# Sliding-window attention on one core: pairs of scores with banks of their own, maxima in two halves

## The chip, the core and the metric

The kernel runs on one core of a Trainium2 chip, as one launch. Its time is the device time of that core in microseconds. A core has a matmul engine (PE, with its weight loads shown apart as PEld), a vector engine (DVE), an activation engine (ACT), a general one (POOL), and a queue that issues transfers (SP). Matmuls write PSUM, a small memory of eight banks of 512 fp32 columns in 128 partitions; DVE and ACT read it. All other tiles lie in SBUF.

## The reference

`x` has 2048 tokens of 512 features. Its layernorm `xn` goes two ways: through attention with 32 heads of 16 features, in which a token sees itself and the 255 tokens before it, and through a mixer block that gates the result. The attention part, from the reference:

```python
qkv = (x @ wqkv).reshape(B, S, 3, H, Dh)            # B=1, S=2048, H=32, Dh=16; x is layernorm(A_x)
scores = einsum("bhqd,bhkd->bhqk", q, k) * Dh ** -0.5
mask = (i - j >= 0) & (i - j < 256)
p = softmax(where(mask, scores, -1e9))
o = einsum("bhqk,bhkd->bhqd", p, v)
s = o.transpose(0, 2, 1, 3).reshape(B, S, D) @ wo
g = silu(gelu(layernorm(x) @ w1 + b1) @ w2 + b2)
out = A_x + s * g
```

## The kernel before

The program has three stages. The first (to about 67 us) normalises and transposes `x` and projects the first heads. The second is the attention loop. The third, after it, is the mixer's second matmul, the output projection and the gate.

The attention loop works on groups of four heads (8 groups, `n`), in blocks of 128 tokens (16 blocks a group). One step `t` of the loop is one block of one group, so steps 0 to 127. Four heads are two **pairs** `p`; the two heads of a pair, `a` = 0 and 1, lie in two halves of 64 partitions. A step has these parts, in this order on PE:

- `prob_block(..., 1)`: scores of pair 1, keys by queries, two matmuls of up to 384 columns, one a head, into the two banks of the tile `stb`. ACT takes the exponential of both (one instruction on 128x768 elements) into `pt`, and POOL masks its two edges (`affine_select`).
- `max_block`: for the block 12 steps ahead (`LEAD`), scores the other way round, queries by keys, to get each query's maximum: four matmuls of 256 columns into the two banks of `xy` (the nearer keys) and four of 128 into columns 0 to 255 of the two banks of `zo` (the farthest block, which only counts where the nearest is masked). The first two blocks of a group have no farthest block and use a constant. DVE puts the masked elements in place (`copy_predicated`, reading `zo`, writing `xy`) and takes the maximum over `xy` (`tensor_reduce`) into `mt`. Every fourth step `max_rows` sends the maxima through DRAM into the rows of the queries, so that a later step's scores come out with the maximum taken off.
- `fill_in(t, 0)`: the first half of this step's **fill**, matmuls that have nothing to do with the step: projections of later groups, values, hidden units of the mixer. They write the banks `fb`. Most steps have six matmuls of 512 columns (or twelve of 256) here.
- planned pieces of other engines (`plan`): casts, splits, fetches.
- `prob_block(..., 0)`: the same for pair 0, again into `stb`.
- `fill_in(t, 1)`: the second half of the fill, between none and twelve matmuls.
- `pv_step`: for the block before, the values: up to 24 small matmuls into the 128 columns `otb`, which are columns 256 to 383 of the second bank of `zo`. ACT copies them out (`oraw`).

Four things hold the order. Each engine works through its instructions in the order in which the program wrote them. `Ordered` (its call is line 42, which all instructions therefore bear in the profile) keeps it so. Waits are put in by the tile layer, by PSUM bank: two engines are never in the same bank of a tile at once, whichever columns they use. And a tile's instructions wait for each other only through the engines' counters; a counter's value names one instruction of that engine.

In the last 12 steps no maxima are left to take, and pair 1's scores use `xy` instead of `stb`.

Of the kernel before, what the change touches and what calls it, by code (L numbers as in the profile page):

```python
# [23 lines left out]
NQ = H // 4  # L24
EPS = 1e-5
NEG = -3.0e38
LEAD = 12
# [22 lines left out]
def mixer_kernel(ctx, tc, x, wqk, wv, wo, w1, b1, w2, b2, out):  # L50


    nc = SimpleNamespace(**{name: Ordered(tc, name) for name in ("tensor", "vector", "scalar", "gpsimd", "sync")})
# [130 lines left out]

    xy = psum.tile([P, 2, 512], F32, name="xy")
    zo = psum.tile([P, 2, 512], F32, name="zo")
    otb = zo[:, 1, 256:384]
    psf = attn.enter_context(tc.tile_pool(name="psf", bufs=1, space=PSUM))
    fb = [psf.tile([P, 512], F32, name=f"fb{i}") for i in range(2)]
    early = ExitStack()  # L190
# [1 line left out]
    stb = []  # L192
# [7 lines left out]
    vt = vp.tile([P, NKB, 16, DH + 1], F32, name="vt")  # L200
# [16 lines left out]
    upper = const.tile([P, P], F32, name="upper")  # L217
    mhalf = const.tile([P, 4], F32, name="mhalf")
    negc = const.tile([P, 1], F32, name="negc")
    nc.vector.memset(upper, 1.0)  # L220
    nc.vector.memset(otb, 0.0)
    for _ in range(16):
        nc.tensor.matmul(zo[:, 0, 0:P], upper, upper, start=True, stop=True)
    nc.gpsimd.memset(mhalf, -0.5)
# [2 lines left out]
    nc.vector.memset(negc, NEG)  # L227
    mask = upper.bitcast(I32).unsqueeze(1).unsqueeze(1).to_broadcast([P, 2, 2, P])
    neg = negc.unsqueeze(2).unsqueeze(2).to_broadcast([P, 2, 2, P])
    b1s = const.tile([P, NF], F32, name="b1s")  # L230


# [234 lines left out]

    mts = {}

    def max_block(n, qb):  # L470

        slot = slots[n % 2]
        if qb % 4 == 0:
# [4 lines left out]
        def scores(p, a, first):  # L478
            r = slice(64 * a, 64 * a + 64)
            out, keys = ((zo[:, a, P * p: P * (p + 1)], slice(P * (qb - 2), P * (qb - 1))) if first else  # L480
                         (xy[:, a, 256 * p + off: 256 * (p + 1)], slice(P * lo, P * (qb + 1))))
            nc.tensor.matmul(out, slot[r, 0, p, P * qb: P * (qb + 1)], slot[r, 1, p, keys], start=True, stop=True)

        for p, a, first in ((0, 1, False), (0, 0, False), (1, 1, False), (1, 0, False),
                            (0, 1, True), (0, 0, True), (1, 1, True), (1, 0, True)):
            if qb >= 2 or not first:
                scores(p, a, first)
        four = xy.rearrange("q a (p k) -> q a p k", p=2)
        nc.vector.copy_predicated(four[:, :, :, 128:256], mask,
                                  neg if qb < 2 else zo[:, :, 0:256].rearrange("q a (p k) -> q a p k", p=2))  # L490
        nc.vector.tensor_reduce(out=mts[n, qb // 4][:, :, :, qb % 4],
                                in_=four[:, :, :, off:256],
                                axis=AX.X, op=ALU.max, negate=True)

    def max_rows(n, c, t):
# [15 lines left out]
    def prob_block(n, kb, p):  # L511
        slot = slots[n % 2]
        w = min(384, S - P * kb)
        pt = pp.tile([P, 2, 384], F32, tag="pt", name=f"pt_{n}_{kb}_{p}")
        both = xy if p and 16 * n + kb + LEAD >= 16 * NQ else stb[0]
        for a in (1, 0):
            r = slice(64 * a, 64 * a + 64)
            nc.tensor.matmul(both[:, a, 0:w], slot[r, 1, p, P * kb: P * (kb + 1)],
                             slot[r, 0, p, P * kb: P * kb + w], start=True, stop=True)
        nc.scalar.activation(pt[:, :, 0:w], both[:, :, 0:w], AF.Exp, scale=DH ** -0.5)  # L520
        nc.gpsimd.affine_select(out=pt[:, :, 0:P], in_=pt[:, :, 0:P], pattern=[[0, 2], [1, P]],
                                compare_op=ALU.is_ge, fill=0.0, base=0, channel_multiplier=-1)
        if w == 384:
            nc.gpsimd.affine_select(out=pt[:, :, 256:384], in_=pt[:, :, 256:384],
                                    pattern=[[0, 2], [-1, P]], compare_op=ALU.is_gt, fill=0.0,
                                    base=0, channel_multiplier=1)
        pts[(n, kb, p)] = pt


    outs = {}  # L530

    def pv_step(n, qb):

        lo = max(qb - 2, 0)
        for kb in range(lo, qb + 1):
            for j in range(4):
                nc.tensor.matmul(otb[32 * j: 32 * j + DH + 1], vt[:, kb, (4 * n + j) % 16],
                                 pts[n, kb, j // 2][:, j % 2, P * (qb - kb): P * (qb - kb + 1)],
                                 start=(kb == lo), stop=(kb == qb),
                                 skip_group_check=True, tile_position=(0, 32 * j))  # L540
        if qb % 4 == 0:
            outs[0] = sgp.tile([P, 512], F32, tag="or", name=f"oraw_{n}_{qb}", bufs=2)
        nc.scalar.copy(outs[0][:, P * (qb % 4): P * (qb % 4 + 1)], otb)
        if qb % 4 == 3:
            (at if n or qb > 7 else behind)(16 * n + qb + 2, nc.sync.dma_start, oT_d[n // 2, n % 2::2, :, P * (qb - 3): P * (qb + 1)], outs[0])

# [228 lines left out]
    def fill_in(t, half):  # L775
        now[:] = t, half
        run(delayed.pop((t, half), ()))
        for fn, args in fills.get((t, half), ()):
            fn(*args)

    end = 16 * NQ
    for t in range(-16, end + 1):
        m = t + LEAD
        if t == -5:
            open_slot(1)
            for k in range(4):
                at(-4 + k, clear_part, k)
        if 0 <= t < end:
            if t == 0:
                early.close()  # L790
                stb.append(attn.enter_context(tc.tile_pool(name="ps_s2", bufs=1, space=PSUM)).tile(
                    [P, 2, 512], F32, name="stb"))
            prob_block(t // 16, t % 16, 1)
        if t >= 0 and m < end:
            max_block(m // 16, m % 16)
        fill_in(t, 0)
        for fn, args in plan.get(t, []):
            fn(*args)
# [12 lines left out]
        for fn, args in ends.get(t, []):  # L811
            fn(*args)
# [20 lines left out]
    for f in range(6, NF, 2):  # L833
        t = gp.tile([P, 2, 512], F32, tag="ohl", name=f"hr_{f}", bufs=4)
# [185 lines left out]
    for c in range(2):  # L1020
# [23 lines left out]
        for i in range(NF + 1):  # L1044
# [47 lines left out]
            k = i - o_from  # L1092
# [163 lines left out]
```

## Time and profile before

| | |
|---|---|
| time, median of 3 runs | 767.51 us (766.88 to 767.55) |
| time of the profiled execution | 767.48 us |
| span of the profiled execution | 765.8 us |
| PE busy, weight loads busy | 745.3 us, 581.8 us |
| DVE, ACT, POOL busy | 526.4, 437.3, 292.3 us |
| first scores of step 0 | 67.22 us |
| first scores of step 116 | 412.24 us |
| end of the last step | about 439.25 us |
| granted PE clock | 1.00 in all stretches |

Idle time of an engine means little by itself here. What counts is which instruction each engine waits for. The span leaves out what lies before the first and after the last profiled instruction (1.7 us here).

### The profile page before, as it was taken

To read this page: it belongs to the slowest core of one execution; us is meant where nothing else is said; L and a number is where in the kernel's file an instruction comes from. 1 tells how busy PE (TensorE), PEld (TensorE's weight loads), DVE (VectorE), ACT (ScalarE), POOL (GpSimd) and SP (SyncE) were. 2 spreads that over 40 slices of the span, in tenths; PEclk is the share of its full clock that TensorE was granted. 3 is DMA by queue.
4 is the path that set the end of the run, shared out by engine and by line. 5 is a ranking of instruction groups with operands and counts; after the bars stand their busy time and mean duration, and the time that the engine had idled before them with its cause. 6 is when DMAs were issued, how large, how long until landed. Compare 5 with 4: busy or idle time off the path is not lost.

```text
span 765.8 us, 18809 instructions
## 1 busy us (share of the span) xinstructions
PE 745.3 (97%) x7428; PEld 581.8 (76%) x7428; DVE 526.4 (69%) x833; ACT 437.3 (57%) x742; POOL 292.3 (38%) x595
## 2 busy tenths in 40 slices
PE   9899999999999999999999999999999999999997
PEld 8777676766768887676676688888878888888886
DVE  6786776877777778887874447753657665676373
ACT  7736767867666676777877755444644553442001
POOL 7612566666565554766766700030101100001102
PEclk9999999999999999999999999999999999999999
DMA  7723455656447863555735283541202322253531
GB/s 261 208 45 75 94 128 137 155 116 134 98 98 219 248 204 98 117 143 145 197 114 155 59 293 120 178 152 56 69 28 93 100 92 81 77 163 115 177 96 55
DMA packets 56951, 99.40 MB, mean 130 GB/s; under 512 B 11104, under 2 KB 11360, under 8 KB 56864
## 3 DMA queue, kind: packets, MB, share of 16 engines
q1 hardware_dynamic: 56864, 98.21, 45.2%
q8 instruction: 58, 0.95, 0.5%
q14 instruction: 29, 0.24, 0.1%
HBM read 51.39 MB, written 29.62 MB: 106 GB/s over the span
## 4 chain that ended last, share of the span: by engine, by line
PE 87%; ACT 4%; DVE 4%; issue 2%; POOL 2%; DMA 1%; SPq 0%; DVEq 0%; ACTq 0%; POOLq 0%
PE acc L42 19%; PE fb L42 18%; PE zo L42 13%; PE p L42 9%; PE stb L42 8%; PE h L42 6%; PE s L42 6%; PE xy L42 5%; ACT pt L42 3%; PE pv L42 2%; DMA x<-in_x_dram 1%; DVE xy L42 1%; DVE mt L42 1%; POOL pt L42 1%; PE yt L42 1%
## 5 line engine op out<-in xcount | busy, mean ns | idle before, releaser
L42 POOL TENSOR_SCALAR_AFFINE_SELECT pt<-pt 128x256 f32<-128x256 f32 x480 | 192.8, 426 | 161.5 <-ACT pt L42 160.4
L42 ACT ACTIVATE pt<-stb 128x768 f32<-128x768 f32 (+1 forms) x244 | 188.6, 773 | 55.5 <-PE stb L42 46.1
L42 DVE TENSOR_REDUCE mt<-xy 128x4 f32<-128x1024 f32 (+1 forms) x128 | 152.6, 1192 | 4.4
L42 PE MATMUL acc<-w,gh 128*128 128x512 f32 x432 | 134.6, 393 | 0.0
L42 DVE COPY_PREDICATED xy<-upper,zo 128x512 f32<-128x512 int32 x112 | 77.5, 692 | 69.1 <-PE zo L42 68.4
L42 PE MATMUL fb<-xnT,wqb 64*128 64x512 f32 (+1 forms) x684 | 115.2, 404 | 0.8 <-DVE xnT L42 0.8
L42 PE MATMUL zo<-pt,vt 128*17 128x128 f32 x2880 | 103.9, 275 | 1.8 <-DVE xy L42 1.3
L42 PE MATMUL stb<-qk 64*128 64x384 f32 (+1 forms) x488 | 96.7, 392 | 7.4 <-ACT pt L42 5.9
L42 POOL TENSOR_TENSOR xo<-xo,gated 128x512 f32<-128x512 f32 x15 | 20.2, 1347 | 219.0 <-DVE gated L42 215.2
L42 PEld LDWEIGHTS zo<-pt,vt 128*17 128x17 f32 x2880 | 67.5, 97 | 39.0 <-issue 17.8
L42 PEld LDWEIGHTS acc<-w,gh 128*128 128x128 f32 x432 | 80.9, 188 | 17.2
L42 PEld LDWEIGHTS stb<-qk 64*128 64x128 f32 x488 | 45.5, 183 | 52.9 <-ACT pt L42 41.6
L42 PE MATMUL acc<-w,gl 128*128 128x512 f32 x216 | 84.4, 391 | 0.0
L42 PEld LDWEIGHTS fb<-xnT,wqb 64*128 64x128 f32 (+1 forms) x684 | 63.4, 186 | 7.8 <-DVE xnT L42 1.2
L42 PE MATMUL xy<-qk 64*128 64x256 f32 (+2 forms) x536 | 61.5, 303 | 2.2 <-DVE mt L42 2.0
L42 ACT COPY oraw<-zo 128x128 f32<-128x128 f32 x128 | 34.1, 266 | 40.2 <-PE zo L42 35.5
L42 PEld LDWEIGHTS xy<-qk 64*128 64x128 f32 x536 | 43.9, 185 | 13.6 <-DVE mt L42 7.1
L42 PEld LDWEIGHTS acc<-w,gl 128*128 128x128 f32 x216 | 40.5, 188 | 9.3 <-DVE gl L42 0.2
L42 ACT ACTIVATE gated<-acc 128x512 f32<-128x512 f32 x16 | 8.7, 595 | 64.8 <-DVE acc L42 64.8
L42 PE MATMUL s<-wos,ohl 128*128 128x512 f32 (+1 forms) x204 | 44.8, 378 | 0.0
L42 PEld LDWEIGHTS s<-wos,ohl 128*128 128x128 f32 x204 | 36.7, 188 | 7.1
L42 ACT COPY p<-p 128x512 f32<-128x512 f32 x21 | 12.3, 584 | 50.1 <-PE p L42 42.6
(190 smaller groups left out, 1191.2 us busy)
## 6 DMA issues: line engine op xcount, KB each, us to landing
qk<-sh SPq DMA_DIRECT2D x128, 128.0 KB
qk<-pjr SPq DMA_DIRECT2D x64, 128.0 KB
oT_d<-oraw SPq DMA_DIRECT2D x32, 256.0 KB
w_d<-in_w_dram SPq DMA_DIRECT2D x14, 512.0 KB
x<-in_x_dram SPq DMA_DIRECT2D x16, 256.0 KB
or<-oT_d SPq DMA_DIRECT2D x16, 256.0 KB
w<-rden_d SPq DMA_DIRECT2D x16, 256.0 KB
xo<-in_x_dram SPq DMA_DIRECT2D x16, 256.0 KB
```

Of the source, the lines that this page charges most:

```text
L42: r = issue(*args, **kwargs)
```

## The change

Three things change in the loop, in all steps from 0 on.

1. Pair 0's scores go to `zo`, columns 0 to 383 of both banks; pair 1's stay in `stb`, in the last 12 steps too.
2. The values go to columns 384 to 511 of the first bank of `stb`, and ACT copies them from there. The memset that clears these columns once stands at step 0, no more at the start.
3. The maxima of a step are taken in two halves, one for each pair (`max_half`): pair 0's where `max_block` stood, pair 1's behind pair 0's scores. Each half is two matmuls into its half of `xy`, two into columns 384 to 511 of both banks of `zo`, a masked copy of half the size and a reduction of half the size. `max_block` remains for the 12 blocks that are done before step 0, with its columns of `zo` moved to 256 to 511.

```diff
-    otb = zo[:, 1, 256:384]
...
-    nc.vector.memset(otb, 0.0)
...
+    mask1 = upper.bitcast(I32).unsqueeze(1).to_broadcast([P, 2, P])
+    neg1 = negc.unsqueeze(2).to_broadcast([P, 2, P])
...
-    def max_block(n, qb):
+    def max_scores(n, qb, places):
...
+        for first in range(1 + (qb >= 2)):
+            for p, firsts in places:
+                for a in (1, 0):
+                    r = slice(64 * a, 64 * a + 64)
+                    out, keys = ((zo[:, a, firsts: firsts + P], slice(P * (qb - 2), P * (qb - 1))) if first else
+                                 (xy[:, a, 256 * p + off: 256 * (p + 1)], slice(P * lo, P * (qb + 1))))
+                    nc.tensor.matmul(out, slot[r, 0, p, P * qb: P * (qb + 1)], slot[r, 1, p, keys],
+                                     start=True, stop=True)
+        return off
...
+    def max_half(n, qb, p):
+
+        off = max_scores(n, qb, ((p, 384),))
+        two = xy[:, :, 256 * p: 256 * (p + 1)]
+        nc.vector.copy_predicated(two[:, :, 128:256], mask1, neg1 if qb < 2 else zo[:, :, 384:512])
+        nc.vector.tensor_reduce(out=mts[n, qb // 4][:, :, p, qb % 4], in_=two[:, :, off:256],
                                 axis=AX.X, op=ALU.max, negate=True)
...
-        both = xy if p and 16 * n + kb + LEAD >= 16 * NQ else stb[0]
+        both = stb[0] if p else zo
...
-                nc.tensor.matmul(otb[32 * j: 32 * j + DH + 1], vt[:, kb, (4 * n + j) % 16],
+                nc.tensor.matmul(stb[0][32 * j: 32 * j + DH + 1, 0, 384:512], vt[:, kb, (4 * n + j) % 16],
...
-        nc.scalar.copy(outs[0][:, P * (qb % 4): P * (qb % 4 + 1)], otb)
+        nc.scalar.copy(outs[0][:, P * (qb % 4): P * (qb % 4 + 1)], stb[0][:, 0, 384:512])
...
+                nc.vector.memset(stb[0][:, 0, 384:512], 0.0)
             prob_block(t // 16, t % 16, 1)
         if t >= 0 and m < end:
-            max_block(m // 16, m % 16)
+            max_half(m // 16, m % 16, 0)
         fill_in(t, 0)
...
             prob_block(t // 16, t % 16, 0)
+        if t >= 0 and m < end:
+            max_half(m // 16, m % 16, 1)
         fill_in(t, 1)
```

How this stands on the engines is shown at three places of step 10. The first is PE from pair 1's scores (the two `stb<-qk` of 384 columns) on: `xy<-qk` and `zo<-qk` of 128 columns are the maxima's, `zo<-pt` the values. The names in brackets are the engines' counters that a matmul waits for. Before:

```order
L42 MATMUL stb<-qk_91 128x384 [waits Activation_49]
L42 MATMUL stb<-qk_91 128x384
L42 MATMUL xy<-qk_706 128x256 [waits DVE_49]
L42 MATMUL xy<-qk_706 128x256 x3
L42 MATMUL zo<-qk_706 128x128 [waits Activation_49]
L42 MATMUL zo<-qk_706 128x128 x3
L42 MATMUL fb_108<-xnT,wqb_1164 128x512
...
L42 MATMUL stb<-qk_91 128x384 [waits Activation_49]
L42 MATMUL stb<-qk_91 128x384
...
L42 MATMUL zo<-pt_8_0_1269,vt 17x128 [waits DVE_49]
```

And in the changed kernel:

```order
L42 MATMUL stb<-qk_91 128x384 [waits Activation_49]
L42 MATMUL stb<-qk_91 128x384
L42 MATMUL xy<-qk_705 128x256 [waits DVE_49]
L42 MATMUL xy<-qk_705 128x256
L42 MATMUL zo<-qk_705 128x128 x2
L42 MATMUL fb_108<-xnT,wqb_1172 128x512
...
L42 MATMUL zo<-qk_91 128x384 [waits DVE_49]
L42 MATMUL zo<-qk_91 128x384
L42 MATMUL xy<-qk_705 128x256 [waits DVE_49]
L42 MATMUL xy<-qk_705 128x256
L42 MATMUL zo<-qk_705 128x128 [waits Activation_49]
L42 MATMUL zo<-qk_705 128x128
```

Before, pair 0's scores waited for ACT, namely for the exponential of pair 1 of the same step. Now they wait for DVE (the first half's masked copy). Behind them the second half has moved in, and its `zo` matmuls wait for ACT, namely for the exponential that reads pair 0's scores.

The second place is PE at the end of the step, from the last values (`<-pt,vt`) to the next step's first scores. Before:

```order
L42 MATMUL zo<-pt_10_0_1363,vt 17x128 [waits Pool_49]
L42 MATMUL zo<-pt_10_0_1363,vt 17x128
L42 MATMUL zo<-pt_10_1_1341,vt 17x128 x2
L42 MATMUL stb<-qk_91 128x384 [waits Activation_49]
L42 MATMUL stb<-qk_91 128x384
```

In the changed kernel:

```order
L42 MATMUL stb<-pt_10_0_1379,vt 17x128 [waits Pool_49]
L42 MATMUL stb<-pt_10_0_1379,vt 17x128
L42 MATMUL stb<-pt_10_1_1361,vt 17x128 x2
L42 MATMUL stb<-qk_91 128x384 [waits Activation_49]
L42 MATMUL stb<-qk_91 128x384
```

The order is the same, but the two now share a tile: the scores' wait for ACT was for the exponential of pair 0 of the step before, and is now for the copy `oraw` of the values just written.

The third place is ACT in the same step. Before:

```order
L42 COPY oraw_8_1335<-zo 128x128 [waits DMAHW1_49,DVE_49,PE_49]
L42 ACTIVATE pt_10_1_1341<-stb 128x768 [waits PE_49,Pool_49]
L42 ACTIVATE pt_10_0_1363<-stb 128x768 [waits PE_49]
L42 COPY oraw_8_1335<-zo 128x128 [waits DVE_49,PE_49]
L42 ACTIVATE pt_11_1_1384<-stb 128x768 [waits PE_49,Pool_49]
```

In the changed kernel:

```order
L42 COPY oraw_8_1355<-stb 128x128 [waits DMAHW1_49,PE_49]
L42 ACTIVATE pt_10_1_1361<-stb 128x768 [waits PE_49,Pool_49]
L42 ACTIVATE pt_10_0_1379<-zo 128x768 [waits DVE_49,PE_49]
L42 COPY oraw_8_1355<-stb 128x128 [waits PE_49]
L42 ACTIVATE pt_11_1_1406<-stb 128x768 [waits PE_49,Pool_49]
```

ACT's order is unchanged. The copy of the values no longer waits for DVE, and the exponential of pair 0 now does.

More of the change, by code (lines that the diff above doesn't have):

```diff
@@ L468, in mixer_kernel @@
     mts = {}
-    def max_block(n, qb):
+    def max_scores(n, qb, places):
         slot = slots[n % 2]
-        if qb % 4 == 0:
+        if qb % 4 == 0 and places[0][0] == 0:
             mts[n, qb // 4] = small.tile([P, 2, 2, 4], F32, tag="mt", name=f"mt_{n}_{qb}")
@@ L476, in max_block @@
         off = 128 * (lo + 1 - qb)
[L478 to L487, printed above, removed]
+        for first in range(1 + (qb >= 2)):
[7 more added lines that the diff above has]
+        return off
+    def max_block(n, qb):
+        off = max_scores(n, qb, ((0, 256), (1, 384)))
         four = xy.rearrange("q a (p k) -> q a p k", p=2)
         nc.vector.copy_predicated(four[:, :, :, 128:256], mask,
-                                  neg if qb < 2 else zo[:, :, 0:256].rearrange("q a (p k) -> q a p k", p=2))
+                                  neg if qb < 2 else zo[:, :, 256:512].rearrange("q a (p k) -> q a p k", p=2))
         nc.vector.tensor_reduce(out=mts[n, qb // 4][:, :, :, qb % 4],
                                 in_=four[:, :, :, off:256],
+                                axis=AX.X, op=ALU.max, negate=True)
+    def max_half(n, qb, p):
[3 more added lines that the diff above has]
+        nc.vector.tensor_reduce(out=mts[n, qb // 4][:, :, p, qb % 4], in_=two[:, :, off:256],
                                 axis=AX.X, op=ALU.max, negate=True)
```

## Prediction

> **What bounds the kernel now.** I read the page's busy shares first, then the stages, then one step of the attention loop instruction by instruction, then the waits. The stages come from the view of busy time by stretch: steps 0 to 115 of the loop run from 67.22 to 412.24 us, steps 116 to 127 to 439.25.
>
> ```profile
> span 765.8 us, 18809 instructions
> PE 745.3 (97%) x7428; PEld 581.8 (76%) x7428; DVE 526.4 (69%) x833; ACT 437.3 (57%) x742; POOL 292.3 (38%) x595
> 67.22:412.24 345.02, 335.10 (x5087) 244.97 (x5087) 268.12 (x371) 246.07 (x423) 216.15 (x471) 1.00 0.55 141
> 412.24:439.25 27.01, 26.52 (x409) 18.38 (x409) 9.77 (x17) 20.25 (x36) 20.14 (x45) 1.00 0.34 102
> ```
>
> The numbers in a stretch's row are its length, the busy time (and count) of PE, weight loads, DVE, ACT and POOL, then the granted clock. PE is busy for 335 of the 345 us, so a step (345.0 / 116 = 2.974 us) is a nearly unbroken line of matmuls, and everything that makes PE wait goes straight into the time. After 439 us the change touches nothing. Step 10, from the timeline, shows the line and the latencies (start, duration, engine, operation, and idle time before it with what ended it):
>
> ```profile
> 97.08 0.44 PE L42 MATMUL stb<-qk 64*128 64x384 f32 x2
> 97.36 0.40 PE L42 MATMUL xy<-qk 64*128 64x256 f32 x4
> 97.59 0.38 PE L42 MATMUL zo<-qk 64*128 64x128 f32 x4
> 97.62 0.81 ACT L42 ACTIVATE pt<-stb 128x768 f32<-128x768 f32 x1
> 97.81 0.92 PE L42 MATMUL fb<-xnT,wqb 64*128 64x512 f32 x6
> 98.07 0.70 DVE L42 COPY_PREDICATED xy<-upper,zo 128x512 f32<-128x512 int32 x1 [0.88 <-PE zo L42]
> 98.48 0.19 PEld L42 LDWEIGHTS stb<-qk 64*128 64x128 f32 x2 [0.19 <-ACT pt L42]
> 98.57 0.35 PE L42 MATMUL stb<-qk 64*128 64x384 f32 x2
> 98.76 0.40 PE L42 MATMUL fb<-xnT,wqb 64*128 64x512 f32 x2
> 98.80 1.23 DVE L42 TENSOR_REDUCE mt<-xy 128x4 f32<-128x1024 f32 x1
> 98.97 0.81 ACT L42 ACTIVATE pt<-stb 128x768 f32<-128x768 f32 x1 [0.53 <-PE stb L42]
> 99.09 0.85 PE L42 MATMUL zo<-pt,vt 128*17 128x128 f32 x24
> 99.87 0.44 PE L42 MATMUL stb<-qk 64*128 64x384 f32 x2
> 100.01 0.27 ACT L42 COPY oraw<-zo 128x128 f32<-128x128 f32 x1 [0.23 <-PE zo L42]
> ```
>
> Four things are to be seen. The step lasts 99.87 - 97.08 = 2.79 us with hardly a hole on PE. From the second pair of scores (98.57) to its exponential (98.97) it is 0.40 us, the exponential takes 0.81. Where the weight load had to wait, it is 97.08 to 97.62, 0.54. And the weight load of 98.48 follows the end of the exponential (97.62 + 0.81 = 98.43) by 0.05 us, so an engine that is waited for lets PE go 0.05 us after it ends. The copy of the values starts 100.01 - 99.09 = 0.92 us after the first value matmul, but PE has gone on at 99.87 and doesn't wait for it: its next user of that bank, `zo`, comes half a microsecond later.
>
> **The change on PE's line.** Call the start of a step's first scores 0. Every place below is a difference of two rows above, or half of one where four matmuls become two.
>
> *The second scores.* First scores to `xy` 0.28; two `xy` matmuls instead of four, 0.23 / 2 = 0.12; two `zo` matmuls instead of four, 0.22 / 2 = 0.11; the fill starts at 0.51 and lasts 98.57 - 97.81 = 0.76. So pair 0's scores can start at 1.27 in `zo`. They wait for the first half's masked copy. That starts 0.37 after its `zo` matmuls (98.07, less the second pair's start at 97.59 + 0.11), so at 0.40 + 0.37 = 0.77. Half a masked copy is not in the trace; the reductions are:
>
> ```profile
> L42 DVE TENSOR_REDUCE mt<-xy 128x4 f32<-128x1024 f32 x110 | 134.8, 1226 | 3.8
> L42 DVE COPY_PREDICATED xy<-upper,zo 128x512 f32<-128x512 int32 x102 | 70.6, 692 | 62.9 <-PE zo L42 62.2
> L42 DVE TENSOR_REDUCE mt<-xy 128x4 f32<-128x512 f32 x7 | 4.9, 693 | 0.2
> L42 DVE COPY_PREDICATED_SCALAR xy<-upper,negc 128x512 f32 x14 | 10.3, 737 | 7.4 <-PE xy L42 7.4
> L42 ACT ACTIVATE pt<-stb 128x768 f32<-128x768 f32 x204 | 165.6, 812 | 49.3 <-PE stb L42 42.0 <-POOL pt L42 1.6 <-POOL xnT L42 0.5
> L42 ACT ACTIVATE pt<-stb 128x512 f32<-128x512 f32 x14 | 8.4, 598 | 3.0 <-PE stb L42 2.3
> L42 ACT ACTIVATE pt<-stb 128x256 f32<-128x256 f32 x14 | 5.4, 385 | 2.7 <-PE stb L42 1.5 <-POOL pt L42 1.0
> L42 ACT COPY oraw<-zo 128x128 f32<-128x128 f32 x115 | 30.6, 266 | 35.1 <-PE zo L42 30.4 <-DVE mt L42 3.8 <-DMA qk<-sh 0.2
> L42 ACT CAST sh<-pjr 128x512 fp32r<-128x512 f32 x28 | 17.1, 612 | 0.0
> ```
>
> (count | busy us, mean ns | idle before.) Half the elements of a reduction save 1226 - 693 = 533 ns, 1.04 ns each, so 256 elements fewer bring the copy from 0.69 to 0.43; its bounds are 0.35 and 0.69. It ends at 1.20, PE may go at 1.25: just under the fill. At its upper bound the scores would start 0.24 later. I take 1.27, and leave open whether the weight load still comes early.
>
> *The wait behind them (the main term).* Directly behind pair 0's scores now stand the second half's `xy` and `zo` matmuls. The `zo` matmuls write the bank that this step's exponential is reading. It starts at 1.27 + 0.40 to 0.54 = 1.67 to 1.81, takes 0.81, and PE goes on 0.05 later: 2.53 to 2.67. Everything else on PE is queued behind: the second fill, the values, the next step. The `xy` matmuls' own wait, for the first half's reduction (1.20 + 0.03 between two of DVE's, 98.77 to 98.80, + 0.69 + 0.05 = 1.97), ends earlier and costs nothing. With 0.11 for the pair and some 0.05 for weights loaded late, the fill starts at 2.69 to 2.83. Today it starts at 98.76 - 97.08 = 1.68. **Cost 1.01 to 1.15 us; I take 1.08.**
>
> *The values in `stb`.* Their copy now reads the bank that the next step's first scores write, and nothing stands between on PE. From the first value matmul it is 0.92 + 0.27 + 0.05 = 1.24 us to the next step, against 99.87 - 99.09 = 0.78 today. **Cost 0.46.**
>
> *What it frees.* The second scores no longer wait for the first exponential, the values no longer for the masked copy. These waits stand in the list of the same stage:
>
> ```profile
> PEld stb L42 <- ACT pt L42: 41.6, 142, 1.3
> PEld zo L42 <- DVE xy L42: 16.1, 51, 0.9
> PE stb L42 <- ACT pt L42: 5.9, 15, 1.0
> PE zo L42 <- DVE xy L42: 1.3, 4, 0.6
> ```
>
> Most of the 41.6 and 16.1 us is weight loading that waits while matmuls run; on the matmuls themselves only 5.9 and 1.3 are left. The mean step is 0.18 over step 10, about half of it longer fills, so at most 0.09 x 116 = 10 us can come back. I take 5.
>
> *DVE and ACT.* DVE's own work in a step grows from 0.69 + 1.23 = 1.92 to 2 x (0.43 + 0.69) = 2.24 us. A step will be over 4 us, so that stays beside PE. ACT does the same work, but what stands between its two exponentials now holds PE. The 612 ns casts of projections, and copies of a fill, are such: the first exponential ends at 0.54 + 0.81 = 1.35, a cast behind it at 1.96, and the second could start at 1.67 to 1.81. That is 0.15 to 0.3 us in some 50 steps: 0 to 15, I take 7. The moved memset is one short instruction before step 0.
>
> **The sum.** Of 116 steps, 14 are the first two blocks of a group (no `zo` in the maxima): there the second half waits only for the first half's reduction. Scores start at 0.28 + 0.12 + 0.76 = 1.16, and the `xy` pair would follow at 1.35. It is held by the half copy (from 0.28 + 0.37, for 0.737 less 256 x 1.04 ns = 0.47), 0.03, the reduction (0.69, or 0.43 in the first block, which has half the keys) and 0.05: to 1.89 or 1.63, 0.41 on average, with the values 0.87. Another 14 are the last two blocks, whose exponentials are 0.21 or 0.43 shorter (rows above): 1.54 - 0.35 = 1.19. The other 88 cost 1.08 + 0.46 = 1.54. In the 12 steps of the tail only the 0.46 stays.
>
> 88 x 1.54 = 135.5; 14 x 0.87 = 12.2; 14 x 1.19 = 16.7; 12 x 0.46 = 5.5; minus 5; plus 7. Together 172 us. The profiled execution took 767.48 us (span 765.8), the median of the runs is 767.51: **939 us**. With every term at its low end it is 88 x 1.47 + 11 + 16 + 5 - 10 = 151, so 919; at its high end 88 x 1.61 + 13 + 18 + 6 + 15 = 194, so 961.
>
> **Rivals.**
>
> *Only one of the two waits is felt (8%).* The order shows that the second half's `zo` matmuls wait for ACT, and if an earlier count of ACT satisfied them, the exponential would be beside the fill and only the 0.46 would remain: 128 x 0.46 = 59, minus 5, so about 820 us. Against it: the only earlier reader of `zo` on ACT is the exponential of the step before, which the masked copy has already waited for, so no wait would be needed then.
>
> *The clock falls (5%).* In every slice and stretch the granted clock is 1.00, with PE never idle for long. In the changed kernel PE stands still for over 1 us and for about 0.5 us in each step of 4.3. If half the clock were granted for half of the stage, the matmul line, 2.79 us a step and 27.0 / 12 = 2.25 in the tail, would add (2.79 x 116 + 2.25 x 12) / 2 = 175 us: about 1110. For it speaks only that such a rhythm is not in this trace; against it, that the holes are short. The Trainium skill ("TensorE: Matmul & The Clock Gate", "A second HAM failure mode: psum-queue depth-cycling") tells of a kernel whose short idle times between groups of matmuls made the clock swing to half, and its section "What's actually happening" gives an idle window of about 3.4 us as what halves it. By the first rule the time would be this rival's, by the second the forecast's; no run here shows a window without matmuls in this stage.
>
> *Faster (3%).* The two score banks end the wait of the second scores for the first exponential. If ACT and DVE were ready at each of the new waits, for instance because PE falls so far behind that both exponentials are done before they are asked for, the freed waits would be all that is left. By the matmuls' own rows that is 5.9 + 1.3 = 7 us, with the weight loads that delay a matmul perhaps 15: 752 to 760. The mechanism decides only where pair 0's exponential ends before PE reaches the second half's `zo` matmuls, 0.33 us after its scores start. It needs 0.40 + 0.81.
>
> *DVE sets the pace (2%).* Its fill copies (0.68 us) could push the first half's copy out so that the `zo` scores start later, at the upper bound of 0.24 a step: 28 us more, 967.
>
> **How the numbers follow.** The forecast holds 82%. Its own spread is 919 to 961, and the unknowns (a half copy of up to 0.69, ACT's queue, weight loads) reach beyond on both sides; 895 to 980 takes in the DVE case, leaves the others out. Slower by over 0.2% (1.5 us, about what a measurement of this kernel can tell): 96%. Faster: 3%. Within: 1%.
>
> **What would show it.** Right: the loop's first 116 steps take some 500 to 515 us in place of 345; on PE's weight loads a large wait `zo` <- ACT `pt` of about 1 us, some 100 times, and one of `stb` <- ACT `oraw` of about 0.4 us; PE's busy share in the stage well under 80%; the half copy near 0.43 us; the clock still 1.00; nothing changed after the loop but its start. Wrong: steps under 4 us with no such wait on `zo`, or a clock below 1.00, or DVE busy without a break while PE waits for it.

## The result and the profile after

The changed kernel takes 966.10 us (961.01, 966.10 and 971.35) against 767.47 us for the kernel before on the same chip: a ratio of 1.259, with a 95% interval of 1.251 to 1.268. A fourth run, slower at a lower clock (981.88 us at 0.913, the others 0.925 to 0.946), is left out of this ratio and of the comparisons below; with it the median is the 968.73 us from which the expectations count. The forecast was 939 us, in a range of 895 to 980. The profiled execution took 971.35 us.

First the page's span, busy shares and slices:

```profile
span 969.6 us, 19162 instructions
PE 844.0 (87%) x7428; PEld 621.9 (64%) x7428; DVE 562.3 (58%) x1065; ACT 437.0 (45%) x742; POOL 289.6 (30%) x595
PE   8998777788777877777788877889999999999997
PEclk9995999857999999999855699999999999999999
```

PE does the same 7428 matmuls as before, and yet is busy 844 us in place of 745. One reason is the clock: in eight of the 40 slices the granted clock is below 0.9, down to 0.5, where it was 1.00 before. It is not the only one, as the next rows show. The busy time by stretch shows which part of the time that is, and where the extra 204 us of span lie (length, PE, weight loads, DVE, ACT, POOL, clock, and the DMA columns):

```profile
68.71:610.35 541.64, 433.26 (x5090) 284.98 (x5091) 304.38 (x602) 245.53 (x423) 215.02 (x473) 0.87 0.35 91
610.35:642.20 31.85, 25.75 (x400) 17.68 (x398) 8.49 (x14) 20.23 (x34) 18.54 (x42) 1.00 0.23 65
268.00:468.00 200.00, 157.56 (x2204) 108.54 (x2204) 122.59 (x246) 94.43 (x163) 81.17 (x187) 1.00 0.40 109
468.00:518.00 50.00, 41.69 (x372) 27.59 (x372) 25.06 (x49) 20.83 (x36) 14.60 (x34) 0.62 0.29 76
```

The first 116 steps take 542 us (345 before), the next eleven, to the first exponential of step 127, 31.9 (25.8 before). What comes after the loop is unchanged. In a stretch at full clock such as 268 to 468, PE is busy for 79% of the time, where it was 97%. Per ordinary step that is still some 3.5 us (0.79 x 4.43, the step time given below) where it was 2.9 (335.10 / 116): even at full clock the same matmuls keep PE busy for longer.

Step 51, at full clock, from the timeline (start, duration, engine, operation, idle time before it and what ended it):

```profile
310.13 0.44 PE L42 MATMUL stb<-qk 64*128 64x384 f32 x2 [0.39 <-ACT oraw L42]
310.42 0.28 PE L42 MATMUL xy<-qk 64*128 64x256 f32 x2
310.53 0.22 PE L42 MATMUL zo<-qk 64*128 64x128 f32 x2
310.59 0.92 PE L42 MATMUL fb<-xnT,wqb 64*128 64x512 f32 x6
310.80 0.43 DVE L42 COPY_PREDICATED xy<-upper,zo 128x256 f32<-128x256 int32 x1 [0.63 <-PE zo L42]
311.26 0.69 DVE L42 TENSOR_REDUCE mt<-xy 128x2 f32<-128x512 f32 x1
311.34 0.37 PE L42 MATMUL zo<-qk 64*128 64x384 f32 x2
311.76 0.81 ACT L42 ACTIVATE pt<-zo 128x768 f32<-128x768 f32 x1 [0.27 <-PE zo L42]
312.01 0.38 PE L42 MATMUL xy<-qk 64*128 64x256 f32 x2 [0.29 <-DVE mt L42]
312.62 0.33 PE L42 MATMUL zo<-qk 64*128 64x128 f32 x2 [0.23 <-ACT pt L42]
312.79 0.44 PE L42 MATMUL fb<-xnT,wqb 64*128 64x512 f32 x2
313.16 0.85 PE L42 MATMUL stb<-pt,vt 128*17 128x128 f32 x24
314.08 0.27 ACT L42 COPY oraw<-stb 128x128 f32<-128x128 f32 x1 [1.51 <-PE stb L42]
314.40 0.44 PE L42 MATMUL stb<-qk 64*128 64x384 f32 x2 [0.39 <-ACT oraw L42]
```

PE stops three times: 0.29 us for the first half's reduction, 0.23 more for pair 0's exponential (312.57 its end, 312.62 the next matmul), 0.39 for the copy of the values. The list of waits (engine and tile, what it waited for: us in total, times, longest) has all three, on the matmuls (PE) and on the weight loads ahead of them (PEld):

```profile
PEld stb L42 <- ACT oraw L42: 88.7, 126, 0.9
PEld zo L42 <- ACT pt L42: 59.6, 100, 1.3
PEld xy L42 <- DVE mt L42: 57.5, 116, 0.9
PE stb L42 <- ACT oraw L42: 48.3, 125, 0.5
PE zo L42 <- ACT pt L42: 36.2, 92, 1.1
PE xy L42 <- DVE mt L42: 28.1, 92, 0.5
```

**Where the clock fell.** At half clock are the stretches 70.25 to 97.56, 114.63 to 118.04, 186.31 to 230.68 and 479.85 to 548.12 us, each a multiple of 3.413 us long to the second decimal. These are the 3.41 us ahead of each fall, and, in the last two rows, the last 3.41 us ahead of two of the rises:

```profile
66.84:70.25 3.41, 1.89 (x13) 1.00 (x12) 2.32 (x7) 1.61 (x4) 0.66 (x2) 1.00 0.03 5
111.22:114.63 3.41, 2.00 (x33) 1.27 (x32) 1.99 (x4) 2.37 (x4) 1.53 (x4) 1.00 0.13 28
182.90:186.31 3.41, 2.27 (x39) 1.50 (x38) 2.17 (x4) 1.56 (x3) 1.36 (x4) 1.00 0.02 2
476.44:479.85 3.41, 2.24 (x23) 1.43 (x18) 1.79 (x4) 2.38 (x4) 1.24 (x4) 1.00 0.54 139
...
227.27:230.68 3.41, 3.02 (x34) 1.66 (x32) 1.51 (x5) 0.27 (x1) 0.00 (x0) 0.50 0.50 103
544.71:548.12 3.41, 3.37 (x36) 1.86 (x32) 2.76 (x5) 1.65 (x3) 3.01 (x5) 0.50 0.24 58
```

PE was busy for 1.89 to 2.27 us of the 3.41 before a fall (55 to 67%), and for 3.02 and 3.37 before these rises.

From the start of one of pair 1's exponentials to the next, the 116 steps sort as follows: at full clock, 69 of the 88 ordinary ones with 4.43 us on average (3.00 in the kernel before), 11 of the first-two-block steps with 3.60 (2.88), 10 of the last-two with 4.03 (2.90); at half clock an ordinary step takes 6.46.

### The profile page after: what moved, and what is told of

Read it like the earlier page. It is cut to its first block, busy times and chain, and to the rows that moved or that the text cites. A ratio compares the mean times of both kernels' runs of the same rounds, so it can differ in the third digit from the quotient of the medians.

```text
span 969.6 us, 19162 instructions
## 1 busy us (share of the span) xinstructions
PE 844.0 (87%) x7428; PEld 621.9 (64%) x7428; DVE 562.3 (58%) x1065; ACT 437.0 (45%) x742; POOL 289.6 (30%) x595
## 4 chain that ended last, share of the span: by engine, by line
PE 73%; ACT 14%; DVE 6%; issue 3%; DMA 2%; POOL 1%; SPq 1%; ACTq 0%; DVEq 0%; POOLq 0%
PE stb L42 17%; PE acc L42 15%; PE fb L42 14%; ACT pt L42 9%; PE p L42 7%; PE zo L42 6%; PE h L42 5%; PE s L42 5%; ACT oraw L42 3%; PE xy L42 3%; DVE mt L42 2%; DVE xy L42 2%; PE pv L42 1%; ACT sh L42 1%; SPq L42 1%
## 5 line engine op out<-in xcount | busy, mean ns | idle before, releaser
L42 DVE COPY_PREDICATED xy<-upper,zo 128x256 f32<-128x256 int32 (+1 forms) x214 | 94.4, 441 | 211.9 <-PE zo L42 211.8
L42 DVE TENSOR_REDUCE mt<-xy 128x2 f32<-128x512 f32 (+3 forms) x244 | 171.1, 701 | 8.4
L42 PE MATMUL zo<-qk 64*128 64x128 f32 (+1 forms) x704 | 115.2, 325 | 36.7 <-ACT pt L42 36.2
L42 ACT ACTIVATE pt<-stb 128x768 f32<-128x768 f32 (+2 forms) x128 | 98.9, 772 | 84.6 <-PE stb L42 80.9
L42 PEld LDWEIGHTS zo<-qk 64*128 64x128 f32 x704 | 73.9, 206 | 77.7 <-ACT pt L42 59.6
L42 PE MATMUL stb<-pt,vt 128*17 128x128 f32 x2880 | 117.0, 299 | 1.7 <-ACT pt L42 1.6
L42 PE MATMUL xy<-qk 64*128 64x256 f32 (+1 forms) x512 | 89.6, 352 | 28.7 <-DVE mt L42 28.1
L42 ACT ACTIVATE pt<-zo 128x768 f32<-128x768 f32 (+2 forms) x128 | 99.0, 773 | 26.7 <-PE zo L42 25.8
L42 PE MATMUL stb<-qk 64*128 64x384 f32 (+2 forms) x256 | 60.6, 470 | 50.0 <-ACT oraw L42 48.3
L42 PEld LDWEIGHTS stb<-pt,vt 128*17 128x17 f32 x2880 | 73.0, 104 | 40.1 <-issue 27.4
L42 PEld LDWEIGHTS acc<-w,gh 128*128 128x128 f32 x432 | 80.9, 188 | 17.1
```

The source lines that it names most:

```text
L42: r = issue(*args, **kwargs)
```

## The experiments

Each was timed beside the kernel before on the same chip (whose median there is 766.98 or 767.2 us). "Full clock" below counts steps whose granted clock was over 0.97.

### 1. Idle matmuls in the hole

```diff
+            for _ in range(4):
+                nc.tensor.matmul(stb[0][:, 1, 384:512], ident, ident, start=True, stop=True)
             max_half(m // 16, m % 16, 1)
```

> The changed kernel with four more matmuls of 128x128 (identity by identity, into columns of `stb` that nothing reads) between pair 0's scores and the second half of the maxima, in the 116 steps with maxima. Nothing is left out. They are there to keep PE busy inside the hole in front of the second half's `zo` matmuls: 4 x 0.11 us (six such matmuls in the first stage took 0.83 us, of which the last one's latency is 0.28), in a hole that at full clock is some 1 us. Theory A, the clock follows how busy PE is: in the changed kernel the clock fell to one half after stretches of 3.41 us in which PE's busy share was 0.56 to 0.67; with 0.44 us more of work in a step of 4.43 the share rises by 0.10, above these, the clock stays at 1.00 in the whole loop, an ordinary step stays at 4.43 us since the added work lies in the hole, and the time falls from 969 to about 926 us, though PE does more. Theory B, the clock falls for another reason (how often PE stops, or the pattern of waits, which this leaves as it is): the mean clock stays between 0.91 and 0.95, and the time at 960 to 985. If the added matmuls were not hidden, an ordinary full-clock step would be 4.5 to 4.9 us.

959.14 us, 1.250 times before (1.248 to 1.252), at a mean clock of 0.996 to 0.998 in all four runs. So the clock did stay up (one fall, in the last 12 steps, where nothing was added), but the time fell by 7 us only (966.10 to 959.14). The timeline of one step says why:

```profile
328.78 1.16 PE L42 MATMUL stb<-ident 128*128 128x128 f32 x8
328.89 0.81 ACT L42 ACTIVATE pt<-zo 128x768 f32<-128x768 f32 x1 [0.25 <-PE zo L42]
329.87 0.39 PE L42 MATMUL xy<-qk 64*128 64x256 f32 x2
330.09 0.22 PE L42 MATMUL zo<-qk 64*128 64x128 f32 x2
```

Four matmuls stand there as eight, 1.09 us from their start to the next matmul in place of my 0.44 (the "six" that I had priced them by were three). The exponential ended at 329.70, the `zo` matmuls came at 330.09. Ordinary steps took 4.59 us, and those of the first two blocks, which have no such hole, 4.36. The clock stayed up as theory A has it, but the step grew too, so that a longer step is left as another reason; the next experiment takes it away.

### 2. Two of them, only where there is a hole

```diff
+        if t >= 0 and m < end and m % 16 >= 2:
+            for _ in range(2):
+                nc.tensor.matmul(stb[0][:, 1, 384:512], ident, ident, start=True, stop=True)
```

> As the first experiment, with two added matmuls of 128x128 instead of four, and only in the 102 steps whose second half has a `zo` part. Nothing is left out. In the first experiment each added matmul stood in the trace as two, so the four took 1.1 us instead of 0.44 and outlasted the hole: the clock stayed at 1.00 but a step grew by 0.16 us where there is a wait for the exponential and by 0.76 where there is none. Two take some 0.55 us and end before the exponential does (0.55 + 0.23 for the `xy` matmuls, in a hole of about 1.2). Theory A, the clock follows PE's busy share: a mean clock of 0.98 to 1.00, ordinary steps of 4.43 to 4.48 us, and 925 to 940 us, which is the cost of the waits alone. Theory B, the clock of the first experiment stayed up because of the longer step or another accident: a mean clock of 0.92 to 0.96 and 950 to 980 us.

928.33 us (927.16 to 936.27), 1.212 times before (1.208 to 1.218); the clock was 0.998 to 1.000 in the three runs below 929, 0.987 in the fourth. In the profiled run it was 1.00 throughout:

```profile
68.74:566.74 498.00, 443.95 (x5498) 306.72 (x5499) 304.03 (x602) 244.12 (x424) 214.97 (x473) 1.00 0.38 99
566.74:598.62 31.88, 25.78 (x402) 17.70 (x400) 8.49 (x14) 20.22 (x35) 18.55 (x42) 1.00 0.24 69
```

Ordinary steps took 4.44 us, first-two-block steps 3.59, last-two 4.08: those of the changed kernel at full clock (4.43, 3.60, 4.03), so the added 204 matmuls cost next to nothing. With more work the kernel is 38 us faster (966.10 to 928.33), and the step is no longer than it was. The change's waits cost 928 - 767 = 161 us, and the other 38 us are the clock. The changed kernel's own steps agree: the profiled run had 27.3 + 3.4 + 44.4 + 68.3 = 143 us at half clock, of which an ordinary step loses 2.03 in 6.46; 143 x 0.314 = 45, and 971 - 45 = 926.

### 3. The halves alone, in the old banks

Against the changed kernel, the main lines:

```diff
-        off = max_scores(n, qb, ((p, 384),))
+        off = max_scores(n, qb, ((p, 128 * p),))
...
-        both = stb[0] if p else zo
+        both = xy if p and 16 * n + kb + LEAD >= 16 * NQ else stb[0]
...
-        nc.scalar.copy(outs[0][:, P * (qb % 4): P * (qb % 4 + 1)], stb[0][:, 0, 384:512])
+        nc.scalar.copy(outs[0][:, P * (qb % 4): P * (qb % 4 + 1)], otb)
```

> The kernel before with the third part of the change alone: the maxima in two halves, pair 0's where the whole stood, pair 1's behind pair 0's scores. The banks are the old ones: both pairs' scores in `stb`, the maxima's farthest blocks in columns 0 to 255 of `zo`, the values in columns 256 to 383 of its second bank. Nothing is left out. Theory, the halves cost by themselves because both use the same banks of `xy` and `zo`: pair 0's scores wait for pair 1's exponential (1.40 to 1.60 us after the first scores), the second half's `xy` matmuls for the first reduction (1.97), and the values for the second half's masked copy (2.08 + 0.37 + 0.43 + 0.05 = 2.93, where today they start at 2.01): an ordinary step is 0.9 us longer than the 2.97 of before, and 102 such and 14 shorter ones of 0.4 make about 865 us, the clock at 1.00. So over half of the loss would come from the halves alone, and the new banks would add the rest by the two waits on ACT. Rival, the halves cost nothing by themselves and all of the loss is the two new waits on ACT: 767 to 790 us.

858.08 us (857.98 to 858.26), 1.118 times before (1.117 to 1.120), clock 1.00. The halves cost 91 us with no new bank at all, as the theory has it (865 us, an ordinary step longer by 0.9 us; it is 0.84). Ordinary steps take 3.84 us, first-two-block steps 3.11, last-two 3.91. One step, and the stage as a whole (its columns as above):

```profile
286.19 0.39 PE L42 MATMUL xy<-qk 64*128 64x256 f32 x2 [0.21 <-DVE mt L42]
286.42 0.22 PE L42 MATMUL zo<-qk 64*128 64x128 f32 x2
286.68 0.43 DVE L42 COPY_PREDICATED xy<-upper,zo 128x256 f32<-128x256 int32 x1
287.17 0.85 PE L42 MATMUL zo<-pt,vt 128*17 128x128 f32 x24 [0.53 <-DVE xy L42]
67.82:503.93 436.11, 383.79 (x5090) 247.24 (x5090) 300.86 (x604) 248.50 (x423) 214.41 (x473) 1.00 0.43 113
```

Second half behind the first reduction (0.21 us), values behind the second masked copy (0.53): two of the waits expected. The new banks end the second of these, and put both ACT waits in their place, at 928 - 858 = 70 us more. In this layout the banks can't be tried without the halves: 384 columns of scores and the 256 of the whole maxima don't fit into one bank of 512.

The last row bears on the busy time. At a clock of 1.00 throughout, PE is busy for 384 us with the matmuls that kept it busy for 335 before. The first two rows show how. From the two `xy` matmuls, behind a stop, it is 0.23 us to the next, as long as from four of them in the unbroken line of step 10; and the two `zo` matmuls, ahead of a stop, count with 0.22 us, where four of them took 0.22 to the next. What a stop costs is thus more than the idle time shown.

### 4. Without the second half's far block

```diff
-        off = max_scores(n, qb, ((p, 384),))
+        off = max_scores(n, qb, ((p, 384),), far=p == 0)
...
-        nc.vector.copy_predicated(two[:, :, 128:256], mask1, neg1 if qb < 2 else zo[:, :, 384:512])
+        nc.vector.copy_predicated(two[:, :, 128:256], mask1, neg1 if qb < 2 or p else zo[:, :, 384:512])
```

> The changed kernel with pair 1's maxima taken without their farthest block: the second half has its two `xy` matmuls, a masked copy from a constant and its reduction, but no `zo` matmuls, and so no wait for pair 0's exponential. Two matmuls a step and that part of pair 1's maxima are left out. Theory, PE is held in two layers there: the second half's `xy` matmuls wait for the first half's reduction, and its `zo` matmuls, 0.6 us later, for the exponential. Taking the second away leaves the first: in step 51 of the changed kernel the `xy` matmuls start at 312.01 and the fill at 312.79; the fill would then start at some 312.24. That is 0.55 us less in 102 steps, 56 us: 870 us with the clock at 1.00, 915 with it as it was, ordinary steps of 3.9 us, and `xy` <- DVE `mt` the largest wait left beside `stb` <- ACT `oraw`. Rival 1, the wait for the exponential is all there is, and the whole 1.08 us goes: ordinary steps of 3.4 us, some 815 us. Rival 2, neither holds the step: 4.4 us as before.

870.12 us, 1.134 times before (1.131 to 1.138), clock 0.988 to 0.999. Ordinary steps at full clock take 3.81 us: 0.63 less than the 4.44 of experiment 2, of which 0.11 are the matmuls left out. This is near the theory's 3.9 us, not the 3.4 us of the first rival or the 4.4 of the second. The step shows the layer below:

```profile
302.07 0.81 ACT L42 ACTIVATE pt<-zo 128x768 f32<-128x768 f32 x1 [0.31 <-PE zo L42]
302.31 0.39 PE L42 MATMUL xy<-qk 64*128 64x256 f32 x2 [0.28 <-DVE mt L42]
302.53 0.51 PE L42 MATMUL fb<-wva,xnT 64*128 64x256 f32 x6
```

The fill now runs beside the exponential, but it still stands behind the reduction (0.28 us).

### 5. The second half behind the fill

```diff
+        fill_in(t, 1)
         if t >= 0 and m < end:
             max_half(m // 16, m % 16, 1)
-        fill_in(t, 1)
```

> The changed kernel with the second half of the maxima moved behind the second fill: pair 0's scores, fill, second half, values. Nothing is left out. Theory, the second half's `zo` matmuls hold PE until pair 0's exponential has ended (the main term of the sum): the fill, 0.41 us on average (none in 20 steps, up to 0.95), now runs inside that wait instead of behind it, and the step falls by all of it, from 4.43 to about 4.0 us at full clock; 116 x 0.41 = 47 us, so 969 - 47 = 922 us with the clock as it was, and near 880 if the busier PE keeps its clock at 1.00. `zo` <- ACT `pt` stays the releaser, with a shorter wait. Rival 1, what holds the step is the amount of work on DVE or ACT and not this wait: the step stays at 4.4 us, the time within 10 us of 969 but for the clock. Rival 2, the chain of the maxima through the banks of `xy` (two halves, each matmuls, masked copy and reduction, with the exponential between) sets the pace: then the step falls to no less than some 3.8 us and a wait `xy` <- DVE `mt` appears ahead of the first half.

899.87 us, 1.171 times before (1.168 to 1.174), clock 0.977 to 0.991. Ordinary steps at full clock took 4.08 us, 0.36 less than in experiment 2 (0.41 expected), those of the first two blocks 3.36 and of the last two 3.77. `PE zo <- ACT pt` fell from 36.2 to 24.1 us. The fill fits into the wait, the time lies in the middle of the theory's 880 to 922, and the denser steps held the clock better. Neither rival shows: matmuls of `xy` waited 9.7 us in all for `mt`.

### 6. The values ahead of the fill

```diff
         if t >= 0 and m < end:
             max_half(m // 16, m % 16, 1)
+        early_values = t >= 1 and t not in as_before
+        if early_values:
+            pv_step((t - 1) // 16, (t - 1) % 16)
         fill_in(t, 1)
...
-        if t >= 1:
+        if t >= 1 and not early_values:
             pv_step((t - 1) // 16, (t - 1) % 16)
```

> The changed kernel with the values moved ahead of the second fill, in all but 20 of the 116 steps (and 4 of the last 12), in which the order stays as it was: pair 0's scores, second half, values, fill. Nothing is left out. Theory, the next step's first scores wait for the copy of the values out of their shared bank (the second term of the sum, 0.46 us): the fill then covers that wait, as far as it is long enough, 0.33 us a step on average (the fill's length, at most 0.46). 96 x 0.33 = 32 us: 969 - 32 = 937 us with the clock as it was, some 895 if it stayed at 1.00. The waits `stb` <- ACT `oraw` of the matmuls fall from 48 us to under 20. Rival, that wait costs nothing by itself since DVE or the exponentials hold the step anyway: the time stays within 10 us of 969 and another wait takes its place, `xy` <- DVE `mt` or `zo` <- ACT `pt`.

913.97 us, 1.190 times before (1.186 to 1.195), clock 0.973 to 0.988. In the ordinary steps that were changed, a full-clock step takes 4.14 us against 4.41 for the same steps in experiment 2; in those left as they were, 4.56 against 4.55. So 0.28 us a step, with 0.33 expected, and `PE stb <- ACT oraw` fell from 48.3 us to 17.1. The second term of the sum is real, and the fill can hide most of it.

### 7. Values, second half, fill

```diff
+        early_values = t >= 1 and t not in as_before
+        if early_values:
+            pv_step((t - 1) // 16, (t - 1) % 16)
         if t >= 0 and m < end:
             max_half(m // 16, m % 16, 1)
         fill_in(t, 1)
...
-        if t >= 1:
+        if t >= 1 and not early_values:
             pv_step((t - 1) // 16, (t - 1) % 16)
```

> The changed kernel with the values moved ahead of the second half, and the fill behind it (pair 0's scores, values, second half, fill) in all but 20 of the 116 steps, in which the order stays as it was. Nothing is left out. Now the 0.85 us of values run inside the wait for pair 0's exponential, and the second half and the fill inside the wait for the copy of the values: both waits of the sum are covered by work. Theory, what is then left is the chain through `xy` and `zo`: from the first half's `xy` matmuls 0.97 us to pair 0's scores (fill, or masked copy), 0.45 to the exponential, 0.81, 0.05, then the second half's `zo` matmuls, 0.37, its masked copy 0.43, 0.03, its reduction 0.69, 0.05 to the next step's `xy`: 3.85 us a step, with `xy` <- DVE `mt` ahead of the first half as the largest wait. 96 x 0.58 = 56 us less than the changed kernel: 870 us with the clock at 1.00, up to 890 if it falls at times. Rival, the two waits on ACT were all that the change costs: steps of 3.1 to 3.3 us and some 810 us.

906.38 us, 1.182 times before (1.178 to 1.186), clock 0.979 to 0.991: above the theory's 870 to 890, far from the rival's 810. The mechanism is there. The changed ordinary steps at full clock take 3.81 us, with 3.85 expected, and the list of waits names the chain:

```profile
PE xy L42 <- DVE mt L42: 77.6, 118, 1.3
PE stb L42 <- ACT oraw L42: 10.7, 28, 0.5
PE zo L42 <- ACT pt L42: 6.6, 24, 0.7
```

With both ACT waits covered, the first half's `xy` matmuls wait for the second half's reduction of the step before (two halves in one pair of banks, with the exponential between them). What I missed are the 20 steps in the old order: a full-clock ordinary one of them takes 5.34 us, against 4.55 in experiment 2, since it begins behind the late reduction of a changed step and ends with its values in the open. 20 x 0.79 is 16 us. The theory also took its 0.58 us off the steps of the first two and the last two blocks, which came to 3.77 and 3.98 us (3.59 and 4.08 in experiment 2), and in the profiled run 27 us were at half clock; together these about make up the distance from 870 to 906.

### 8. Pair 0's exponential in two instructions

```diff
+        cuts = (0, 192, w) if p == 0 and w == 384 else (0, w)
+        for c0, c1 in zip(cuts, cuts[1:]):
+            nc.scalar.activation(pt[:, :, c0:c1], both[:, :, c0:c1], AF.Exp, scale=DH ** -0.5)
```

> The changed kernel with pair 0's exponential made in two instructions of 384 elements each in place of one of 768, in the steps in which it has 768. Nothing is left out. By the rows of 768 and 512 elements (812 and 598 ns) an element costs 0.83 ns and an instruction 0.17 us by itself, so the two take 0.98 us, 0.17 more. Theory, this exponential is what holds the second half's `zo` matmuls: ordinary steps at full clock grow by 0.17 us (4.43 to 4.60), the steps of the first two blocks stay at 3.60; 88 x 0.17 = 15 us. PE's busy share in a step falls with it, so the clock falls oftener than in the changed kernel: a mean clock of 0.89 to 0.92, in all 985 to 1010 us. Rival, the exponential has slack: ordinary steps at full clock stay at 4.43, the time at 960 to 980.

The four runs took 956.2, 957.3, 984.7 and 999.8 us at clocks of 0.961, 0.959, 0.917 and 0.894. They differ so much with the clock that the totals settle nothing, and only steps at full clock are compared here. In the profiled run (999.8 us) such an ordinary step takes 4.48 us, 0.05 more than the changed kernel's 4.43, where 0.17 was expected. But the pair of instructions was not 0.17 us longer. The group by shape, and two of them in the timeline:

```profile
L42 ACT ACTIVATE pt<-zo 128x384 f32<-128x384 f32 x224 | 97.8, 491 | 32.6 <-PE zo L42 32.0
...
253.66 0.88 ACT L42 ACTIVATE pt<-zo 128x384 f32<-128x384 f32 x2
```

Each takes 0.49 us, both together 0.88, 0.07 more than the one of 0.81. The step grew by about as much as the exponential did, which is what a wait without slack gives. 0.05 in 4.43 is small, but it stands only where it should: step by step at full clock in both kernels, 52 ordinary steps grew by 0.05 on average, and eight first-two-block steps, whose exponential is split too but has no `zo` matmuls waiting behind it, by 0.01. The clock forecast (0.89 to 0.92, for 985 to 1010 us) missed two of the four runs, which kept 0.96 and stayed below even the rival's 960 to 980 us.

## Why the prediction came out as it did

The time was 27 us above the forecast and inside its range, by two errors of opposite sign: the waits cost 161 us where the sum had 172, and the clock, which the forecast left at 1.00, added 38. The range was drawn to leave a falling clock out, so that the time lies in it with one is in part luck. The mechanism of the main sum, two new waits on ACT, is what the runs show.

- **The main wait** was found where it was forecast, and its size was a little off. In step 51 pair 0's scores start 1.21 us after the first scores (1.27 forecast), their exponential at 1.63 (1.67 to 1.81), the `zo` matmuls at 2.49 (2.53 to 2.67), the fill at 2.66 (2.69 to 2.83): 0.98 us later than in step 10 of before, where the sum has 1.08. The half copy was 0.43 us as estimated. Of the 0.10 between them, 0.06 is that the scores start earlier (the fill begins at 0.46, not 0.51), and the rest that the exponential follows them by 0.42, near the lower end of the 0.40 to 0.54 that the forecast left open. (It put these two values down to whether the weight load had to wait; but in step 10 both loads had waited, 0.21 us the first and 0.19 the second.)
- **What "costs nothing" meant there.** The forecast said that the `xy` matmuls' own wait for the reduction ends earlier and costs nothing. It is hidden, but only by the wait above it: of the 0.98 us, its part runs first. This is most likely why the `zo` weight loads waited 0.60 us on average (59.6 us, 100 times) and not the announced 1 us, and why taking the exponential's wait away gave back 0.52 us beside the matmuls left out (experiment 4). The forecast's words would let a reader expect all of it back (the 3.4 us of experiment 4's first rival).
- **The values in `stb`** cost what was forecast: from first value matmul to next scores 314.40 - 313.16 = 1.24 us, to the second decimal, and 0.55 us a step in the last steps (6.1 us in eleven; 0.46 forecast). Experiment 6 shows it as a cost of its own.
- **The smaller terms.** First-two-block steps cost 0.71 (0.87 forecast), last-two 1.18 (1.19). An ordinary step costs 4.44 - 3.00 = 1.44 = 0.98 + 0.46, so the 5 us freed and the 7 us for ACT's casts are not visible beside the two waits, and no run tells them apart. (In the term for the last two blocks the sum takes 0.35 us off; the mean of its 0.21 and 0.43 is 0.32, which makes 0.4 us in all.) By the steps of experiment 2: 88 x 1.44 + 14 x 0.71 + 14 x 1.18 + 12 x 0.55 = 160 us, and the loop starts 1.0 us later.
- **The clock is the step that failed.** It was the second rival, held at 5% and about 1110 us, and what spoke against it was "that the holes are short". Short holes were enough: filling them brought the clock back to 1.00 with the step unchanged (experiment 2). But that rival's price was wrong too: not half the stage but 143 of its 542 us were at half clock in the profiled run, and there an ordinary step grew by 2.03 us and not by its matmul line's 2.79. Part of the slower matmuls runs inside the waits, and ACT's instructions take no longer there (0.81 and 0.27 us in the step that starts at 198.18); this is argued, not tested by itself. In all the clock makes 38 us, not 175.
- **The other rivals.** That only one wait is felt is out: both stand in the list, and experiments 4 to 6 move them one by one. Faster is out too. DVE's pace is not the bound of the changed kernel, but it waits close by: the chain through `xy` and its reductions is what is left once the ACT waits are covered (experiment 7).
- **Of the signs announced,** the two waits, the half copy and the unchanged rest came. The 116 steps took 542 us, not 500 to 515, and 498 with the clock held up. PE's share in the stage was 80% and not well below, and 79% in the stretch at full clock: the matmuls before a stop count for longer, as experiment 3 shows at a clock of 1.00, and a lower clock makes all of them longer. So lost time hides in a busy share in two ways.

What the forecast didn't ask is how much of the loss belongs to which part: 91 us come with the halves alone, 70 with the banks, 38 with the clock. None of the orders tried, nor the halves alone, is faster than the kernel before.

## What to carry to other kernels

Where a line of matmuls bounds a kernel, place each new sharing of a bank on that line and write down what is queued behind it: reader's start, its length, and the release are the price, less whatever independent work stands between. Waits lie in layers, so price what remains when the uppermost is gone. And when holes open in a dense line of matmuls, the clock may answer (here it did, but not in experiment 3): look at the granted clock of each stretch before reading a busy share, and separate its part by filling the holes with matmuls that nothing needs.

## What the runs showed of the hardware that was not expected

**Half the clock without a single long hole.** Before the falls of the changed kernel PE was busy for 55 to 67% of 3.41 us, in pieces, with no hole above 1.3 us. The share alone is no sharp threshold: stretches of that length with 61 to 66% also stayed at full clock, and in experiments 5 to 8 a few falls came after shares of 0.70 to 0.82. Half-clock stretches ended after shares of 0.885 or more, and some after such a share did not end. In experiment 3, where no stretch of that length had less than 0.69, the clock stayed at 1.00. What else decides stays open. The Trainium skill ("TensorE: Matmul & The Clock Gate", "What's actually happening") gives a free-running window of 3413 ns, and the traces agree: half-clock stretches are multiples of it. By its rule that an idle window halves the clock these falls would not have come; its section "A second HAM failure mode: psum-queue depth-cycling" tells of such a swing in another kernel, from short idle times between groups of matmuls, and this trace agrees.

**More matmuls, less time.** 204 matmuls whose results nothing reads made the changed kernel 38 us faster (966.10 to 928.33).

**Two ACT instructions overlap.** Two exponentials of 384 elements, 0.491 us each, took 0.88 us back to back, so a split costs 0.07 us and not the 0.17 by which the rows of different sizes price an instruction. The Trainium skill ("Perfetto Trace Analysis", "Optimizing Scalar/DVE Operations") has it that part of a profiled latency overlaps with the next instruction, and this row agrees.
